# Threshold attention and a gated feed-forward: q and k loaded once and rearranged on the chip, in place of two shifted loads

## The chip, the cores and the metric

The kernel runs on one core of a Trainium2 chip. The metric is device microseconds (us) of one execution, start of the first instruction to end of the last. Before the change the median of three runs is 576.11 us (573.69 to 577.81). The profile shown is of one execution with a span of 573.6 us between its first and last instruction.

The engines are named as the profile names them: PE (TensorE matmul), PEld (its weight loads), DVE (VectorE), ACT (ScalarE), POOL (GpSimd) and SP (SyncE, which here only issues transfers). SPq and ACTq are their instruction queues as issuers of DMA.

## The reference

Eight batches, eight heads, 576 rows (tokens) of 64 numbers each. Attention keeps only the scores that lie within `tau` = 0.02 of the largest of their row; a feed-forward block follows.

```python
scores = q @ k.T / sqrt(64)                       # per batch and head, 576 x 576
thresh = max(scores, row) - tau
attn   = softmax(where(scores >= thresh, scores, -1e9))
x      = (attn @ v) -> [4608 tokens, 8 heads * 64]
xn     = x / sqrt(mean(x*x) + 1e-6) * rms_g
out    = (silu(xn @ w_gate) * (xn @ w_val)) @ w_out      # 512 -> 1536 -> 512
```

Inputs and output are float32.

## The kernel before

**Tiling.** Two heads form a pair (four pairs a batch). A chunk is 128 rows of q of one batch, four chunks a batch; the last 64 rows of two batches make one more chunk together. That is 36 chunks, and with four pairs each 144 steps. One step runs through these instructions:

- Scores: PE multiplies a chunk of q with all 576 k rows, each head on 64 of the 128 partitions of `qkt` (L687), into `s_ps`.
- DVE copies the scores, negated and scaled, to `ssb` (three buffers) and takes the row minimum, `mx` (L720).
- POOL adds tau: `nth` (L761), a tiny instruction.
- ACT pushes everything beyond the threshold far away (Prelu with a huge slope, L772, two a step) and takes the exponential, into `wsb` in float16 (L779, three buffers).
- The weights must be transposed for the next product. In the first 16 steps PE does it (L824); in the other 128 a transposing DMA does, from SP's queue (L839), into `wt` (five buffers).
- PE multiplies two steps' weights with v (L857 and L862); DVE divides by the row sums (L879, L881 or L886) into `xsb`.

After four pairs of a chunk, ACT squares (L903), POOL finds the root mean square and scales (L906, L908, L911: the norm chain), and SP issues a transposing DMA into `xnT` (L915). Four chunks (two at first) form a group for the feed-forward block: PE for gate (L974) and value (L979), ACT for tanh (L988), DVE for the products (L991, L996), PE for the output (L1045; L1020 in the last group), DVE or ACT for the copy out (L1058, L1060), and SP or ACT for the store (`store_blocks`, L948, for blocked batches). The feed-forward matmuls fill PE while the softmax chain runs.

**q and k.** For the scores they must lie with the 64 numbers of a head along partitions, so each has to be transposed. Batches 0 and 1 are transposed on PE (L338, L448). Batches 2 to 7 are "blocked": DVE's transpose turns each 32x32 block in place (block of partitions by 32 columns), and does not move blocks between groups of 32 partitions. A row of q has two halves of 32 numbers, so the second halves must already lie on another block of partitions than the first. The kernel before obtains that by loading every row twice: each block of 32 partitions holds 18 whole rows per partition (`RUN = 18`, 4608 bytes in one run), one copy (`e = 0`) stored 32 elements later than the other (`e = 1`). The reading view `kx`, `qx` takes 32 of each 64 columns at one place for all partitions, and so finds first halves on one block and second halves on the next:

```python
rows = slice(64 * h + 32 * e, 64 * h + 32 * e + 32)
at = WIDE * (1 - j) + 32 * (1 - e)
nc.sync.dma_start(out=qkx[rows, at:at + GROUP * RUN * D]..., in_=src[b, a0:a0 + GROUP]...)
```

A load covers two pairs of one side of the partitions; four loads (h, e) bring two pairs of k, four more those of q. There is one buffer for each of k and q, so the next two pairs' loads wait until the turns of the present two have read it (L373; turns at L387, L392 and L397, the last for q). Which rows sit where decides the row order of everything that follows, so v and the output are loaded and stored in the same order: v in four loads of 32 partitions a batch, the output in four stores of 32 rows a chunk.

**Order.** Every instruction is put in its engine's list by a planner that knows a cost for each (`COST`, `DMA_NS`), buffers, and a rank per kind of operation (`RANK`). The lists are fixed when the kernel is built, and each engine works strictly through its own. All loads and nearly all stores share SP's list with the transposing DMAs.

Of the kernel before, what the change touches and what calls it, by code (L numbers as in the profile page):

```python
# [9 lines left out]
FP16 = mybir.dt.float16  # L10
# [10 lines left out]
    sp=420.0, sp_v=600.0, sp_w=600.0, sp_tr=1300.0, sp_qk=680.0, sp_tl=630.0, sp_qb=600.0, turn=600.0, turn_t=210.0, turn_q=680.0,  # L21
)
DMA_NS = dict(qkb=750.0, qk=1250.0, tl=700.0, v=880.0, vt=350.0, wt=1700.0, xt=800.0, out=800.0, w=820.0, wo=2500.0)
# [3 lines left out]
    ACT={"emit_ffn/ev": 300, "emit_ffn/store": 50, "emit_ffn/tanh": -293, "emit_k_tail/ev": -150, "emit_q_tail/ev": -130, "emit_qk/ev": 320,  # L27
        "emit_softmax/ex2": -329.5, "emit_softmax/prelu": 80, "emit_x/sq": -310},
    DVE={"emit_av/half": -20, "emit_blocks/turn_k": 30, "emit_blocks/turn_kt": 30, "emit_blocks/turn_q": 68, "emit_burst/ttr": -40, "emit_ffn/ev":
        103, "emit_ffn/gate": -60, "emit_ffn/silu": -20, "emit_k_tail/ev": -120, "emit_qk/ev": -80, "emit_softmax/ev": 360},  # L30
    PE={"emit_av/fn": -270, "emit_burst/fn": -140, "emit_ffn/gmm": 19, "emit_ffn/omm": 21, "emit_ffn/vmm": -110, "emit_k_tail/tr": 240,
        "emit_q_tail/tr": -160, "emit_qk/tr": 90, "emit_softmax/tr": -120},
    POOL={"emit_softmax/nthr": -90, "emit_x/mean": -80, "emit_x/norm": -20, "round_/<lambda>": -30, "main/<lambda>": 690, "main/cast": -220},
# [115 lines left out]
def kernel(  # L149
# [12 lines left out]
    nc = tc.nc  # L162
# [16 lines left out]
    def ps(name, n):  # L179
# [10 lines left out]
    RUN = S // 32  # L190
    LEAD = TAIL // 32
    GROUP = 2
    WIDE = GROUP * RUN * D + 32
    qkx = sb("qkx", [128, 2 * WIDE])
    kx, qx = [qkx[:, WIDE * j + 32:WIDE * (j + 1)].rearrange("p (a r d) -> p a r d", a=GROUP, d=D)[:, :, :, 0:32] if 0 else
              bass.AP(tensor=qkx.tensor, offset=qkx.offset + WIDE * j + 32, ap=[list(qkx.ap[0]), [RUN * D, GROUP], [D, RUN], [1, 32]])
              for j in range(2)]
# [20 lines left out]
    esb = [sb(f"esb{i}", [128, S], FP16) for i in range(NES)]  # L218
# [139 lines left out]

    assert BLOCKED == 2 and WIDE < 1024 * NQK
    turned = []  # L360

    def emit_block_loads(b, g, prio):

        los = {}
        for j, src in ((1, k), (0, q)):
            before = turned[j] if turned else [x for t in tr_of for x in t[-NQK:]] + ([] if j else tail_load["use", 0])
            for h in range(2):
                for e in range(2):
                    def load(o, j=j, src=src, h=h, e=e):
                        rows = slice(64 * h + 32 * e, 64 * h + 32 * e + 32)  # L370
                        at = WIDE * (1 - j) + 32 * (1 - e)
                        a0 = NP * h + GROUP * g
                        nc.sync.dma_start(out=qkx[rows, at:at + GROUP * RUN * D].rearrange("s (a n) -> s a n", a=GROUP),  # L373
                                          in_=src[b, a0:a0 + GROUP].rearrange("a (s r) d -> s a (r d)", r=RUN))

                    pr = prio + BLOCK_STEP * len([x for y in los.values() for x in y])
                    los.setdefault(j, []).append(gated(add("SP", COST["sp_qb"], pr, before, load, dma=DMA_NS["qkb"], bulk=True), pr))
                    los[j][-1].lat = LAT_QB
        turned[:] = [[], []]
        return los  # L380

    def emit_blocks(b, p, prio, los):
        free = last_s.get(("k", b - 2, p), [])
        dst = qkt[b % 2][:, p]

        def turn_k(o):
            nc.vector.transpose(out=dst[:, TAIL:S].rearrange("p (c k d) -> p c k d", c=4, d=32),  # L387
                                in_=kx[:, p % GROUP, LEAD:RUN].rearrange("p (k c) d -> p c k d", c=4))

        def turn_kt(o):  # L390
            src = kx[:, p % GROUP, 0:LEAD]
            nc.vector.transpose(  # L392
                out=dst[:, 0:2 * S].rearrange("p (j n) -> p j n", j=2)[:, :, 0:TAIL].rearrange("p j (t d) -> p j t d", d=32),
                in_=bass.AP(tensor=src.tensor, offset=src.offset, ap=[list(src.ap[0]), [0, 2], list(src.ap[1]), list(src.ap[2])]))

        def turn_q(o):
            nc.vector.transpose(out=dst[:, S + TAIL:2 * S + TAIL].rearrange("p (r d) -> p r d", d=32), in_=qx[:, p % GROUP])  # L397

        tk = gated(add("DVE", COST["turn"], prio, los[1] + free, turn_k), prio)
        tt = gated(add("DVE", COST["turn_t"], prio, los[1] + free, turn_kt), prio)  # L400
        tq = gated(add("DVE", COST["turn_q"], prio, los[0] + free, turn_q), prio)
        turned[0].append(tq)
        turned[1] += [tk, tt]
        for c in range(4):
            qk_ready[b, p, c] = [tk, tt, tq]
        kt_ready[b, p] = []
# [155 lines left out]
    def emit_v(b, prio):  # L562
# [13 lines left out]
        for p in range(NP):  # L576
            pr = prio + 3 * p if b else (-25.0, -24.0, -21.0, -20.0)[p]
            n = len(v_cast)
            nat = vst[n % len(vst)]

            def load(o, p=p, nat=nat):
                nc.sync.dma_start(out=nat, in_=main[:, 2 * p:2 * p + 2])

            if b < BLOCKED:
                lo = [gated(add("SP", COST["sp_v"], pr, v_cast[n - len(vst):n - len(vst) + 1] if n >= len(vst) else [], load,
                                dma=DMA_NS['v'], bulk=True), pr)]
            else:
                nat = vst8.rearrange("q (h a) x -> q a h x", h=2)[:, p]
            if b >= BLOCKED and p == 0:
                lo = []  # L590
                for g in range(4):
                    def load_block(o, g=g):
                        at = LEAD + 4 * g
                        nc.sync.dma_start(out=vst8[32 * g:32 * g + 32].rearrange("s h (c d) -> s h c d", d=D),
                                          in_=v[b].rearrange("h (s r) d -> s h r d", r=RUN)[:, :, at:at + 4])

                    pl = pr + V_FROM + V_STEP * g
                    lo.append(gated(add("SP", COST["sp_v"], pl, v_cast[-NP:], load_block, dma=DMA_NS['v'], bulk=True), pl))
                    lo[-1].lat = LAT_V
            ca = add("POOL", COST["cast_v"], (pr + V_CAST if b >= BLOCKED else pr + 1 if b else p - 1.0), lo + free(p), round_(  # L600
                t[:, p, 0:8, 0:D].rearrange("q (c h) d -> q h c d", h=2),
                nat.rearrange("q h (c d) -> q h c d", d=D)))
            v_cast.append(ca)
            v_ready.setdefault((b, p), []).append(ca)
            if p == 0:
                def load_tail(o):
                    for e in range(2):
                        if b >= BLOCKED:
                            for t in range(LEAD):
                                at = 64 * e + 32 * t  # L610
                                nc.sync.dma_start(out=vtl[at:at + 32], in_=v[b, NP * e:NP * e + NP].rearrange(
                                    "a (s r) d -> r s a d", r=RUN)[t])
                            continue
                        nc.sync.dma_start(out=vtl[64 * e:64 * e + 64], in_=hv[e, MAIN:S])

                lt = gated(add("SP", (4 if b >= BLOCKED else 2) * COST["sp_tl"], pr + 0.3, vt_cast[-2:], load_tail, dma=DMA_NS['vt'], bulk=True), pr + 0.3)
# [228 lines left out]
    def emit_av(s):  # L845
# [31 lines left out]
        def half(_):  # L877
            o3 = ring[o.slot[0]][:, 0:4 * (D + 1)].rearrange("p (h d) -> p h d", d=D + 1)
            nc.vector.reciprocal(out=r, in_=o3[:, :, D])  # L879
            if bs[0] >= BLOCKED:  # L880
                nc.vector.tensor_tensor(  # L881
                    out=xsb[ci % 2].rearrange("p (h a d) -> p a h d", h=2, d=D)[:, 2 * hp:2 * hp + 2],
                    in0=o3[:, :, 0:D].rearrange("p (a h) d -> p a h d", h=2),
                    in1=r.rearrange("p (a h) -> p a h", h=2)[:, :, :, None].to_broadcast([128, 2, 2, D]), op=ALU.mult)
                return
# [59 lines left out]

    def store_blocks(b, oi, n, row, at, late):
        for i in range(n):
            (nc.scalar if late and i % 2 else nc.sync).dma_start(  # L948
                out=out[b * S:b * S + S].rearrange("(s r) d -> r s d", r=RUN)[row + i], in_=osb[oi][at + 32 * i:at + 32 * i + 32])

    def emit_ffn(slot, parts, ready_step, pace, streamed):
# [81 lines left out]
        for j, (ci, _) in enumerate(parts):  # L1033
# [28 lines left out]
            def store(o, oi=oi, kind=kind, b=b, c=c, late=late):  # L1062
                if kind == "m":
                    if b >= BLOCKED:
                        store_blocks(b, oi, 4, 4 * c, 0, late)
# [3 lines left out]
                else:  # L1069
                    for e in range(2):  # L1070
                        if 2 * b >= BLOCKED:
                            store_blocks(2 * b + e, oi, LEAD, MAIN // 32, 64 * e, False)
                            continue
                        r0 = (2 * b + e) * S
                        nc.sync.dma_start(out=out[r0 + MAIN:r0 + S], in_=osb[oi][64 * e:64 * e + 64])
# [5 lines left out]
            osb_use[oi] = add("ACT" if late else "SP", (2200.0 if b >= BLOCKED else COST["sp"]) if kind == "m" else 2100.0 if 2 * b >= BLOCKED else 1100.0, pr, [e], store,  # L1081
# [140 lines left out]
BLOCK_STEP = 0.6  # L1222
# [50 lines left out]
```

## Time and profile before

| what | value |
|---|---|
| median time | 576.11 us (573.69 to 577.81, three runs) |
| span of the profiled execution | 573.6 us, mean granted clock 0.988 |
| busy: PE / DVE / ACT / POOL | 529.8 (92%) / 468.0 (82%) / 445.2 (78%) / 129.5 us (23%) |
| DMA moved | 103.21 MB; SP's queue 100.18 MB, its packets 91.9% of 16 engines' span |
| q/k loads of blocked batches | 96 of 288 KB, median 5.3 (k) and 5.7 us (q) to landing |
| transposing DMAs | 128 for wt, median 4.6 us, and 36 for xnT, 4.2 us |
| turns (L387, L392, L397) | 24 of each at 698, 287 and 765 ns |

Shares of busy time are averages over stages that are limited by different things: until about 80 us the weights of the feed-forward block come in and are rounded, from 80 to 440 us the blocked batches' q and k come in, and after about 516 us only feed-forward work is left. So it is the stretches that have to be read, and in them the waits. DMA shares count the time that packets take, and packets overlap, so a share can exceed 1.

### The profile page before, as it was taken

What the parts mean: (1) busy time and instruction counts of PE and PEld (TensorE: products, weight loads), DVE (VectorE), ACT (ScalarE), POOL (GpSimd) and SP (SyncE); (2) the same over time, 40 slices, a digit from 0 to 9 for tenths busy, and PEclk for the clock granted to TensorE, in tenths of its full rate; (3) what the DMA queues carried; (4) which work ended last, traced back from release to release, by engine and by line L of the source; (5) the groups of instructions that cost most, each with busy time, mean ns of one, the idle gap of its engine ahead of it and who ended that gap; (6) DMA issues with size and microseconds to landing.
All of it is one profiled execution on the core that took longest, in us unless ns stands there. A gap on an engine that the chain in (4) does not pass through costs nothing.

```text
span 573.6 us, 14361 instructions
## 1 busy us (share of the span) xinstructions
PE 529.8 (92%) x5336; PEld 276.2 (48%) x5336; DVE 468.0 (82%) x1342; ACT 445.2 (78%) x648; POOL 129.5 (23%) x334
## 2 busy tenths in 40 slices
PE   8998999886999998989998989988989999999994
PEld 4666765443544444435453535443444454454441
DVE  4998988775999798989997989987789888866641
ACT  5998988678997998878986998886788999952210
POOL 2378402041221312113121311231120411111000
PEclk9999999988999999999999999998999999999998
DMA  8999999999799999999999999998999885761103
GB/s 195 242 262 277 202 158 211 196 223 218 154 214 200 204 202 171 205 219 215 192 217 213 183 206 178 226 197 182 195 199 224 149 131 111 128 113 44 31 19 93
DMA packets 222887, 103.21 MB, mean 180 GB/s; under 512 B 199264, under 2 KB 208992, under 8 KB 222816
## 3 DMA queue, kind: packets, MB, share of 16 engines
q1 hardware_dynamic: 219984, 100.18, 91.9%
q0 software_dynamic: 1600, 1.57, 1.9%
q8 instruction: 42, 0.69, 0.6%
q10 hardware_dynamic: 1232, 0.52, 0.4%
q14 instruction: 29, 0.24, 0.2%
HBM read 51.91 MB, written 9.44 MB: 107 GB/s over the span
## 4 chain that ended last, share of the span: by engine, by line
PE 41%; DMA 26%; ACT 17%; DVE 6%; issue 5%; POOL 3%; SPq 0%; ACTq 0%; DVEq 0%; POOLq 0%
DMA wt<-wsb 21%; PE s_ps L687 11%; ACT ssb L772 8%; PE ring L1045 8%; PE ring L974 7%; PE ring L979 6%; ACT wsb L779 6%; DVE ssb L720 4%; DMA xnT<-xn 2%; PE ring L862 2%; ACT th L988 2%; DMA stg<-in_moe_w_val_dram 2%; PE s_ps L1020 2%; PE ring L857 1%; PE s_ps L979 1%
## 5 line engine op out<-in xcount | busy, mean ns | idle before, releaser
L772 ACT ACTIVATE ssb<-ssb,nth 128x576 f32<-128x576 f32 x288 | 209.6, 765 | 23.4 <-POOL nth L761 22.9
L779 ACT ACTIVATE wsb<-ssb 128x1152 f16<-128x1152 f32 x144 | 166.8, 1159 | 30.6 <-DMA wt<-wsb 28.8
L720 DVE CUSTOM_DVE_ANT_0 ssb<-s_ps,zrow 128x576 f32<-128x576 f32 (+8 forms) x288 | 170.7, 635 | 9.3 <-PE s_ps L687 6.8
L687 PE MATMUL s_ps<-qkt 64*64 64x288 f32 (+9 forms) x2240 | 171.9, 415 | 5.0 <-DVE mxp L720 3.8
L974 PE MATMUL ring<-xnT,wg 128*128 128x512 f16 (+1 forms) x464 | 109.9, 360 | 5.5 <-DMA xnT<-xn 5.5
L687 PEld LDWEIGHTS s_ps<-qkt 64*64 64x64 f32 (+1 forms) x2240 | 80.9, 135 | 70.6 <-issue 27.6
L979 PE MATMUL ring<-xnT,wv 128*128 128x512 f16 (+1 forms) x456 | 107.9, 359 | 0.3 <-DVE hf L996 0.3
L988 ACT ACTIVATE th<-ring 128x512 f32<-128x512 f32 (+1 forms) x116 | 62.8, 542 | 44.2 <-PE ring L974 44.0
L991 DVE SCALAR_TENSOR_TENSOR sl<-th,ring 128x512 f32<-128x512 f32 (+1 forms) x116 | 71.9, 624 | 17.8 <-ACT th L988 17.7
L761 POOL TENSOR_SCALAR nth<-mx 128x2 f32<-128x2 f32 x144 | 31.0, 215 | 244.0 <-DVE mx L720 240.3
L720 DVE CUSTOM_DVE_ANT_0 ssb<-s_ps,zrow,mxp 128x128 f32<-128x128 f32 (+7 forms) x112 | 53.2, 510 | 21.2 <-PE s_ps L687 18.4
L974 PEld LDWEIGHTS <-wg 128*128 128x128 f16 x480 | 44.1, 98 | 54.6 <-issue 14.1
L979 PEld LDWEIGHTS <-wv 128*128 128x128 f16 x480 | 43.8, 98 | 55.0 <-issue 17.3
L862 PE MATMUL ring<-va,wt 128*128 128x65 f16 (+1 forms) x1280 | 53.5, 193 | 0.0
L857 PE MATMUL ring<-va,wt 128*128 128x130 f16 (+1 forms) x160 | 32.5, 227 | 20.5 <-DMA wt<-wsb 20.5
L862 PEld LDWEIGHTS <-wt 128*128 128x128 f16 (+1 forms) x1280 | 47.1, 100 | 4.3
L1045 PE MATMUL ring<-wo,hf 128*128 128x512 f16 x204 | 47.9, 379 | 0.0
L1045 PE MATMUL ring<-wo,stg 128*128 128x512 f16 x156 | 38.5, 392 | 0.0
L996 DVE TENSOR_TENSOR stg<-ring,sl 128x512 f16<-128x512 f32 (+1 forms) x57 | 35.5, 625 | 2.3
L996 DVE TENSOR_TENSOR hf<-ring,sl 128x512 f16<-128x512 f32 (+1 forms) x57 | 35.3, 623 | 2.1 <-PE ring L979 0.4
L857 PEld LDWEIGHTS <-wt 128*128 128x128 f16 (+1 forms) x160 | 14.2, 99 | 40.1 <-DMA wt<-wsb 23.7
L1045 PEld LDWEIGHTS <-hf 128*128 128x128 f16 x216 | 20.1, 98 | 24.6 <-issue 2.5
(69 smaller groups left out, 403.6 us busy)
## 6 DMA issues: line engine op xcount, KB each, us to landing
qkx<-in_k_dram SPq DMA_DIRECT2D x48, 288.0 KB, 5.3
qkx<-in_q_dram SPq DMA_DIRECT2D x48, 288.0 KB, 5.7
vst<-in_v_dram SPq DMA_DIRECT2D x32, 256.0 KB, 4.6
out_dram<-osb SPq DMA_DIRECT2D x98, 64.0 KB, 1.8
stg<-in_moe_w_gate_dram SPq DMA_DIRECT2D x6, 512.0 KB, 6.2
stg<-in_moe_w_val_dram SPq DMA_DIRECT2D x6, 512.0 KB, 6.3
wt<-wsb SPq DMA_TRANSPOSE x128, 4.6
out_dram<-osb SPq DMA_DIRECT2D x8, 256.0 KB, 3.6
```

Source lines behind the costliest of these rows:

```text
L687: nc.tensor.matmul(s_ps[h][rows, at:at + hi - lo], lhs(hs), k_of(bb, p, h)[hs, lo:hi], start=True, stop=True)
L720: nc.vector.tensor_tensor_reduce(out=ssb_of(s)[:, h, lo:hi], in0=s_ps[h][:, at:at + hi - lo], in1=zrow[:, lo:hi], scale=-1.0 / 8.0, scalar ...
L772: nc.scalar.activation(out=sb_[:, h], in_=sb_[:, h], func=PRELU, scale=-1.0, bias=nth[m][:, h:h + 1], **PRELU_KW)
L779: nc.scalar.activation(out=wsb[s % NW], in_=sb_, func=AF.Exp)
L857: nc.tensor.matmul(ring[o.slot[0]][rs, at:at + 2 * (D + 1)], w[:, 4, rs], va[vi][:, p, 8:10].rearrange("p e d -> p (e d)"), start=True, st ...
L862: nc.tensor.matmul(ring[o.slot[0]][rs, at:at + D + 1], w[:, 5 * h + j, rs], va[vi][:, p, 2 * j + h], start=False, stop=(h == 1 and j == 3))
L974: nc.tensor.matmul(ring[o.slot[0]][:, 0:n], wg[d][:, fs], xnT[slot][:, d, 0:n], start=(d == 0), stop=(d == 3))
L979: nc.tensor.matmul(ring[o.slot[0]][:, 0:n], wv[d][:, fs], xnT[slot][:, d, 0:n], start=(d == 0), stop=(d == 3))
L988: nc.scalar.activation(out=th[i][:, 0:n], in_=ring[g.slot[0]][:, 0:n], func=AF.Tanh, scale=0.5)
L991: nc.vector.scalar_tensor_tensor(out=sl[i][:, 0:n], in0=th[i][:, 0:n], scalar=1.0, in1=ring[g.slot[0]][:, 0:n], op0=ALU.add, op1=ALU.mult)
L996: nc.vector.tensor_tensor(out=hf[hi][:, 0:n], in0=ring[vv.slot[0]][:, 0:n], in1=sl[i][:, 0:n], op=ALU.mult)
L1045: nc.tensor.matmul(ring[(first or o).slot[0]], hf[hs[fc][0]][:, 128 * j:128 * (j + 1)], wo[:, fc], start=(fc == 0), stop=(fc == NFC - 1))
```

## The change

Every row of q and k is now loaded once, nine whole rows on each of 128 partitions (`RUN = 9`, 2304 bytes in one run): 64 partitions hold one head, the other 64 the other head of the pair. A load covers two pairs, and there are two buffers (`g`), so that all four pairs of a batch have a place. Both halves of a row now lie on the same partition. To put the halves on the blocks of partitions where the turn needs them, POOL swaps the second halves of one block of 32 partitions with the first halves of the next, by way of a `spare` tile: three copies for each half of a load. The turns by DVE stay, with other shapes.

The row order changes with it (64 x 9 in place of 32 x 18), so v comes in two loads of 64 partitions a batch, its last rows in two loads and not four, and the output in two stores of 64 rows a chunk. Heads of a pair are now neighbours, so the output product needs no form of its own for blocked batches. An unused buffer (`esb`) makes room for `spare`. The planner's costs and ranks are set anew, which changes the order of the lists of all engines.

```diff
-    RUN = S // 32
+    RUN = S // 64
...
-    qkx = sb("qkx", [128, 2 * WIDE])
+    qkx = sb("qkx", [128, 2 * 2 * GROUP * RUN * D])
+    nat = qkx.rearrange("p (g j a r d) -> p g j a r d", g=2, j=2, a=GROUP, d=D)
+    spare = sb("spare", [128, GROUP * RUN * 32]).rearrange("p (a r d) -> p a r d", a=GROUP, d=32)
...
     def emit_block_loads(b, g, prio):
...
+                nc.sync.dma_start(out=own.rearrange("p a r d -> p a (r d)"),
+                                  in_=src[b, a0:a0 + 2 * GROUP].rearrange("(a h) (m r) d -> h m a (r d)", h=2, r=RUN))
...
             for h in range(2):
-                for e in range(2):
...
+                lower, upper = slice(64 * h, 64 * h + 32), slice(64 * h + 32, 64 * h + 64)
+                moves = [(spare[upper], own[lower, :, :, 32:64]), (own[lower, :, :, 32:64], own[upper, :, :, 0:32]),
+                         (own[upper, :, :, 0:32], spare[upper])]
+                last = [lo] + spare_use[-1:]
+                for dst, at in moves:
+                    def swap(o, dst=dst, at=at):
+                        nc.gpsimd.tensor_copy(out=dst, in_=at)
+
+                    last = [add("POOL", COST["swap"], prio + SWAP_AT, last, swap)]
...
         def turn_q(o):
-            nc.vector.transpose(out=dst[:, S + TAIL:2 * S + TAIL].rearrange("p (r d) -> p r d", d=32), in_=qx[:, p % GROUP])
+            nc.vector.transpose(out=dst[:, S + TAIL:2 * S + TAIL], in_=nat[:, g, 1, a].rearrange("p r n -> p (r n)"))
...
-    def store_blocks(b, oi, n, row, at, late):
-        for i in range(n):
...
                     if b >= BLOCKED:
-                        store_blocks(b, oi, 4, 4 * c, 0, late)
+                        rows = out[b * S:b * S + S].rearrange("(m r) d -> r m d", r=RUN)
+                        for i in range(2):
+                            (nc.scalar if late and i else nc.sync).dma_start(out=rows[2 * c + i], in_=osb[oi][64 * i:64 * i + 64])
```

More of the change, by code (lines that the diff above doesn't have):

```diff
@@ L20 @@
     pool_tiny=302.0, pool_mean=944.0, pool_dma=880.0, cast_v=620.0, cast_vt=475.0, cast_w=665.0,
-    sp=420.0, sp_v=600.0, sp_w=600.0, sp_tr=1300.0, sp_qk=680.0, sp_tl=630.0, sp_qb=600.0, turn=600.0, turn_t=210.0, turn_q=680.0,
+    sp=420.0, sp_v=600.0, sp_w=600.0, sp_tr=1300.0, sp_qk=680.0, sp_tl=630.0, sp_qb=600.0, swap=790.0, turn=600.0, turn_t=210.0, turn_q=680.0,
 )
-DMA_NS = dict(qkb=750.0, qk=1250.0, tl=700.0, v=880.0, vt=350.0, wt=1700.0, xt=800.0, out=800.0, w=820.0, wo=2500.0)
+DMA_NS = dict(qkb=1600.0, qk=1250.0, tl=700.0, v=880.0, vt=350.0, wt=1700.0, xt=800.0, out=800.0, w=820.0, wo=2500.0)
 SWITCH = 125.0
 RANK = dict(
[L27 to L33, printed above, removed]
+    ACT={"emit_ffn/ev": 400, "emit_ffn/store": 40, "emit_ffn/tanh": -350, "emit_k_tail/ev": -230, "emit_q_tail/ev": -70, "emit_qk/ev": 390,
+        "emit_softmax/prelu": 170, "emit_x/sq": -320},
+    DVE={"emit_av/half": -39, "emit_blocks/turn_k": 90, "emit_blocks/turn_kt": 140, "emit_blocks/turn_q": 280, "emit_burst/ttr": -50, "emit_ffn/ev":
+        185, "emit_ffn/gate": -20, "emit_ffn/silu": -44, "emit_k_tail/ev": -110, "emit_qk/ev": -120, "emit_softmax/ev": 250},
+    PE={"emit_av/fn": -340, "emit_burst/fn": -110, "emit_ffn/gmm": 21, "emit_ffn/omm": 22, "emit_ffn/vmm": -20, "emit_k_tail/tr": 220,
+        "emit_q_tail/tr": -70, "emit_softmax/tr": -110},
+    POOL={"emit_block_loads/swap": 60, "emit_softmax/nthr": -240, "emit_x/mean": -110, "emit_x/norm": -50, "round_/<lambda>": 60, "main/<lambda>":
+        760, "main/cast": -300},
 )
@@ L189 @@
     wo = sb("wo", [128, NFC, DM], FP16)
-    RUN = S // 32
-    LEAD = TAIL // 32
+    RUN = S // 64
     GROUP = 2
-    WIDE = GROUP * RUN * D + 32
-    qkx = sb("qkx", [128, 2 * WIDE])
-    kx, qx = [qkx[:, WIDE * j + 32:WIDE * (j + 1)].rearrange("p (a r d) -> p a r d", a=GROUP, d=D)[:, :, :, 0:32] if 0 else
-              bass.AP(tensor=qkx.tensor, offset=qkx.offset + WIDE * j + 32, ap=[list(qkx.ap[0]), [RUN * D, GROUP], [D, RUN], [1, 32]])
-              for j in range(2)]
+    qkx = sb("qkx", [128, 2 * 2 * GROUP * RUN * D])
+    nat = qkx.rearrange("p (g j a r d) -> p g j a r d", g=2, j=2, a=GROUP, d=D)
+    spare = sb("spare", [128, GROUP * RUN * 32]).rearrange("p (a r d) -> p a r d", a=GROUP, d=32)
     qkn = [qkx[:, 1024 * i:1024 * (i + 1)].rearrange("p (j c h d) -> p j c h d", j=2, c=4, d=D) for i in range(NQK)]
@@ L217 @@
     nth = [sb(f"nth{i}", [128, 2]) for i in range(6)]
-    esb = [sb(f"esb{i}", [128, S], FP16) for i in range(NES)]
+    esb = [sb(f"esb{i}", [128, S], FP16) for i in range(NES if set(WAYS) != {"pp"} else 0)]
     NW = 3
@@ L357, in emit_qk @@
             qk_ready[b, p, c] = done
-    assert BLOCKED == 2 and WIDE < 1024 * NQK
-    turned = []
+    assert BLOCKED == 2
+    turned, spare_use = {}, []
     def emit_block_loads(b, g, prio):
-        los = {}
+        done = {}
         for j, src in ((1, k), (0, q)):
-            before = turned[j] if turned else [x for t in tr_of for x in t[-NQK:]] + ([] if j else tail_load["use", 0])
-            for h in range(2):
-                for e in range(2):
[L369 to L380, printed above, removed]
@@ new lines, in emit_block_loads, with load @@
+            before = turned[g, j] if (g, j) in turned else [x for t in tr_of for x in t[-NQK:]] + (tail_load["use", 0] if g else [])
+            own = nat[:, g, 1 - j]
+            def load(o, src=src, own=own):
+                a0 = 2 * GROUP * g
+                nc.sync.dma_start(out=own.rearrange("p a r d -> p a (r d)"),
+                                  in_=src[b, a0:a0 + 2 * GROUP].rearrange("(a h) (m r) d -> h m a (r d)", h=2, r=RUN))
+            pr = prio + BLOCK_STEP * (1 - j)
+            lo = gated(add("SP", COST["sp_qb"], pr, before, load, dma=DMA_NS["qkb"], bulk=True), pr)
@@ new lines, in emit_block_loads @@
+            lo.lat = LAT_QB
+            done[j] = []
+            for h in range(2):
+                lower, upper = slice(64 * h, 64 * h + 32), slice(64 * h + 32, 64 * h + 64)
[6 more added lines that the diff above has]
+                    last = [add("POOL", COST["swap"], prio + SWAP_AT, last, swap)]
+                spare_use.append(last[0])
+                done[j] += last
@@ L382, in emit_blocks @@
+            turned[g, j] = []
+        return done
     def emit_blocks(b, p, prio, los):
@@ L384, in emit_blocks @@
         dst = qkt[b % 2][:, p]
+        g, a = divmod(p, GROUP)
         def turn_k(o):
-            nc.vector.transpose(out=dst[:, TAIL:S].rearrange("p (c k d) -> p c k d", c=4, d=32),
-                                in_=kx[:, p % GROUP, LEAD:RUN].rearrange("p (k c) d -> p c k d", c=4))
+            nc.vector.transpose(out=dst[:, TAIL:S].rearrange("p (c k n) -> p c k n", c=4, n=64),
+                                in_=nat[:, g, 0, a, 0:RUN - 1].rearrange("p (k c) n -> p c k n", c=4))
         def turn_kt(o):
[L391 to L394, printed above, removed]
+            src = nat[:, g, 0, a, RUN - 1]
+            nc.vector.transpose(out=dst[:, 0:2 * S].rearrange("p (j n) -> p j n", j=2)[:, :, 0:TAIL],
+                                in_=bass.AP(tensor=src.tensor, offset=src.offset, ap=[list(src.ap[0]), [0, 2], [1, TAIL]]))
         def turn_q(o):
-            nc.vector.transpose(out=dst[:, S + TAIL:2 * S + TAIL].rearrange("p (r d) -> p r d", d=32), in_=qx[:, p % GROUP])
+            nc.vector.transpose(out=dst[:, S + TAIL:2 * S + TAIL], in_=nat[:, g, 1, a].rearrange("p r n -> p (r n)"))
         tk = gated(add("DVE", COST["turn"], prio, los[1] + free, turn_k), prio)
@@ L401, in emit_blocks @@
         tq = gated(add("DVE", COST["turn_q"], prio, los[0] + free, turn_q), prio)
-        turned[0].append(tq)
-        turned[1] += [tk, tt]
+        turned[g, 0].append(tq)
+        turned[g, 1] += [tk, tt]
         for c in range(4):
@@ L578, in emit_v, with load @@
             n = len(v_cast)
-            nat = vst[n % len(vst)]
-            def load(o, p=p, nat=nat):
-                nc.sync.dma_start(out=nat, in_=main[:, 2 * p:2 * p + 2])
+            nat_v = vst[n % len(vst)]
+            def load(o, p=p, nat_v=nat_v):
+                nc.sync.dma_start(out=nat_v, in_=main[:, 2 * p:2 * p + 2])
             if b < BLOCKED:
@@ L587, in emit_v @@
             else:
-                nat = vst8.rearrange("q (h a) x -> q a h x", h=2)[:, p]
+                nat_v = vst8[:, 2 * p:2 * p + 2]
             if b >= BLOCKED and p == 0:
                 lo = []
-                for g in range(4):
+                for g in range(2):
                     def load_block(o, g=g):
-                        at = LEAD + 4 * g
-                        nc.sync.dma_start(out=vst8[32 * g:32 * g + 32].rearrange("s h (c d) -> s h c d", d=D),
-                                          in_=v[b].rearrange("h (s r) d -> s h r d", r=RUN)[:, :, at:at + 4])
+                        nc.sync.dma_start(out=vst8[64 * g:64 * g + 64].rearrange("m h (c d) -> m h c d", d=D),
+                                          in_=v[b].rearrange("h (m r) d -> m h r d", r=RUN)[:, :, 4 * g:4 * g + 4])
                     pl = pr + V_FROM + V_STEP * g
-                    lo.append(gated(add("SP", COST["sp_v"], pl, v_cast[-NP:], load_block, dma=DMA_NS['v'], bulk=True), pl))
+                    lo.append(gated(add("SP", COST["sp_v"], pl, v_cast[-NP:], load_block, dma=2 * DMA_NS['v'], bulk=True), pl))
                     lo[-1].lat = LAT_V
@@ L601, in emit_v @@
                 t[:, p, 0:8, 0:D].rearrange("q (c h) d -> q h c d", h=2),
-                nat.rearrange("q h (c d) -> q h c d", d=D)))
+                nat_v.rearrange("q h (c d) -> q h c d", d=D)))
             v_cast.append(ca)
@@ L607, in load_tail @@
                     for e in range(2):
[L608 to L616, printed above, removed]
+                        nc.sync.dma_start(out=vtl[64 * e:64 * e + 64], in_=hv[e, MAIN:S] if b < BLOCKED else v[b].rearrange(
+                            "(a e) (m r) d -> e r m a d", e=2, r=RUN)[e, RUN - 1])
+                lt = gated(add("SP", 2 * COST["sp_tl"], pr + 0.3, vt_cast[-2:], load_tail, dma=DMA_NS['vt'], bulk=True), pr + 0.3)
                 for e in range(2):
@@ L879, in half @@
             nc.vector.reciprocal(out=r, in_=o3[:, :, D])
[L880 to L885, printed above, removed]
             nc.vector.tensor_tensor(
@@ L944 @@
     clock = [0.0]
-    def store_blocks(b, oi, n, row, at, late):
-        for i in range(n):
-            (nc.scalar if late and i % 2 else nc.sync).dma_start(
-                out=out[b * S:b * S + S].rearrange("(s r) d -> r s d", r=RUN)[row + i], in_=osb[oi][at + 32 * i:at + 32 * i + 32])
     def emit_ffn(slot, parts, ready_step, pace, streamed):
@@ L1070, in store @@
                     for e in range(2):
-                        if 2 * b >= BLOCKED:
-                            store_blocks(2 * b + e, oi, LEAD, MAIN // 32, 64 * e, False)
-                            continue
                         r0 = (2 * b + e) * S
-                        nc.sync.dma_start(out=out[r0 + MAIN:r0 + S], in_=osb[oi][64 * e:64 * e + 64])
+                        dst = out[r0 + MAIN:r0 + S] if 2 * b < BLOCKED else out[r0:r0 + S].rearrange("(m r) d -> r m d", r=RUN)[RUN - 1]
+                        nc.sync.dma_start(out=dst, in_=osb[oi][64 * e:64 * e + 64])
             e = add("DVE" if on_dve else "ACT", 600.0 if on_dve else 476.0, pr - PUSH[0],
@@ L1080, in emit_ffn @@
             late = late and kind == "m"
-            osb_use[oi] = add("ACT" if late else "SP", (2200.0 if b >= BLOCKED else COST["sp"]) if kind == "m" else 2100.0 if 2 * b >= BLOCKED else 1100.0, pr, [e], store,
+            osb_use[oi] = add("ACT" if late else "SP", (1100.0 if b >= BLOCKED else COST["sp"]) if kind == "m" else 1100.0, pr, [e], store,
                               dma=DMA_NS['out'])
@@ L1221 @@
 BLOCKED = 2
-BLOCK_STEP = 0.6
+BLOCK_STEP = 3.0
+SWAP_AT = 4.0
 V_STEP = 1.0
```

## The prediction

> **What bounds the kernel now.** I read the engine shares first, then stretches of the span, then the waits of the middle stretch, then the DMA answers for that stretch and for a quiet one. All "before" figures are from a profiled execution with a span of 573.6 us.
>
> Busy time by stretch (columns: stretch, its length, busy us of PE, PEld, DVE, ACT, POOL with instruction counts, granted clock, DMA share, GB/s):
>
> ```profile
> core 0: us, PE busy (x) PEld busy (x) DVE busy (x) ACT busy (x) POOL busy (x), PEclk, DMA share, GB/s
> 0.00:80.00 80.00, 73.35 (x858) 49.42 (x862) 64.31 (x185) 67.34 (x108) 37.78 (x81) 1.00 1.04 225
> 80.00:440.00 360.00, 331.47 (x3473) 166.97 (x3465) 312.22 (x930) 299.83 (x428) 74.73 (x207) 0.99 1.09 201
> 440.00:574.00 134.00, 124.99 (x1013) 59.80 (x1013) 91.45 (x229) 78.02 (x115) 17.04 (x46) 0.99 0.51 96
> ```
>
> PE is nearest to its limit. Of its 43.8 us of idle time 28.5 (360 - 331.47) lie in 80-440, the stretch in which blocked q and k are loaded and turned; 6.7 are the start and 8.6 the end. In 80-440 the packets in flight fill more than the 16 DMA engines' time (share 1.09, packets overlapping); after 440, with no more q/k loads, the share halves and PE has no gap worth naming until 565.6. The waits of 80-440 (us in total, times, longest):
>
> ```profile
> POOL nth L761 <- DVE mx L720: 178.7, 78, 6.6
> ACT wsb L779 <- DMA wt<-wsb: 27.0, 20, 3.3
> PE ring L857 <- DMA wt<-wsb: 19.8, 20, 2.7
> ACT ssb L772 <- POOL nth L761: 16.8, 21, 2.5
> ACT th L988 <- PE ring L974: 14.6, 12, 2.3
> ```
>
> So 19.8 of PE's 28.5 us end with a transposed weight block (wt) landing, and ACT loses 27.0 to the same transfers, because a wsb buffer is free only once it has been transposed. Now the DMA queue in 80-440 and in the quiet stretch 460-500 (packets, MB, share; issues and median us to landing):
>
> ```profile
> q1 hardware_dynamic: 152167, 71.80, 108.2%
> qkx<-in_q_dram SPq DMA_DIRECT2D x47, 288.0 KB, 5.8
> qkx<-in_k_dram SPq DMA_DIRECT2D x44, 288.0 KB, 5.2
> wt<-wsb SPq DMA_TRANSPOSE x101, 4.9
> xnT<-xn SPq DMA_TRANSPOSE x25, 4.5
> ```
>
> ```profile
> q1 hardware_dynamic: 16925, 4.84, 74.1%
> wt<-wsb SPq DMA_TRANSPOSE x12, 3.4
> ```
>
> The same transpose lands in 3.4 us when no loads run beside it and in 4.9 when they do. That 1.5 us is what the change can get at.
>
> [...] 128x512 casts take 628 ns and 64x256 casts 406, so 0.87 ns [...] an element and 184 ns fixed. [...]
>
> **The change, part by part.**
>
> *q/k loads.* 96 loads of 288 KB (every byte twice) become 24 of 576 KB: 28.3 MB become 14.2. Packet time in 80-440 is 1.082 x 360 = 390 us. In 460-500 it is 0.741 x 40 = 29.6 us for 4.84 MB, nearly all transposes: 6.1 us per MB. The 101 wt and 25 xnT transposes of 80-440 are 33.1 MB, so 202 us; the other 38.7 MB take 188, 4.8 per MB. The 91 q/k loads there (26.8 MB) take 129. Halved at the same price, 65 are saved[...]. The share falls from 1.08 to 0.83-0.90. On a line through (0.74, 3.4 us) and (1.08, 4.9), 0.865 gives 3.95: a wt lands about 0.95 us sooner. PE's 20 waits average 1.0 us, so most shrink to little; since the order on each engine is fixed and ACT (83% busy) and DVE (87%) must now deliver sooner, I take 12 of 19.8. PE's xnT waits there (4.7 in all, L974) give 2 more. Ends: 5 and 22.
>
> *Swaps.* 48 halves of loads times three copies = 144 GpSimd copies of 32x576. From the casts' line: 184 + 576 x 0.87 = 685 ns, plus about 0.09 us from one dependent POOL instruction to the next (norm chain at 189 us): 0.77 us, 111 in all[...]. POOL goes from 75 to about 186 of 360 us: not full. But it is in order, and a swap waits for its load and for the swap before it. Queued behind are nth (L761, for which ACT's prelu waits) and the norm chain (for which the xnT transpose waits). By the built order 101 nth lie between first and last swap; 48 have no swap between them and the nth before, 20 have four to six. Steps come every 3.6 us, and five swaps last 3.9. I put 1.5 us of lateness on those 20 and 0.4 on the other 33: 43 us. Three ssb buffers take up part of it, and PE has feed-forward matmuls meanwhile; I take a third for ACT (14) and a third of that for the end: +5. Ends: 0 and +29.
>
> *Turns.* Same three per pair, same element counts: nothing. They now follow six swaps (4.6 us) per load, hidden while the second group buffer lets loads start earlier; before, a late q load at 400 us stood on the chain.
>
> *Queue.* SP's list falls from 475 to 327 instructions; 72 q/k issues at about 0.48 us and some 76 of v and stores at about 0.42 free about 65 us. SP mostly waits for ACT (98.0 us for L772 alone), so this only makes transposes leave sooner; counted within the 12. At the end it counts by itself: the last matmul ends at 565.6, SP issues six 32-row stores from 566.24 to 569.95 and the last two from 570.05 to 570.89. Half as many: three in 1.9 us and one in 0.4, ending at about 568.5. -2 (1 to 3).
>
> *The rest.* The two output multiplies (L881, L886) both take 425 ns: nothing. esb is not used. PE's rows barely change (7186 to 7194), but with other priorities 264 instead of 228 matmuls stand after the last weight-value product. At about 0.216 us that is 7.8 us of work moved behind 516 us; it is free if the softmax part really ends earlier, and lost if not.
>
> Sum: -12 - 2 + 5 - 2 = -11; 576.1 - 11 = **565**.
>
> **Rivals.** (A) The sum, 565. (B) PE fills nearly all: 80-440 keeps 8 of its 28.5 us of gaps and POOL costs nothing: 576.1 - 20 - 2 = 554. For it: after 440 PE ran without gaps. Against: ACT and DVE are at 83% and 87% there. (C) GpSimd becomes the gate: [...] with -12 - 2 - 2 the time is 589. For it: ACT already waits 16.8 us for nth with POOL at 21%, and a late load now holds nth up too. Against: POOL keeps half its time free. (D) The wait changes its name: 12 saved at wt, 12 lost at nth: 576.1 - 2 = 574, or with the 7.8 us of moved matmuls uncovered 582.
>
> **How the numbers follow.** A 0.48, B 0.22, C 0.18, D 0.12. The time is A's, 565. The range, 549 to 586, takes in most of B, all of D, the near part of C, and A with either end of its DMA term. Faster by over 1% (under 570.3): nearly all of A and all of B, 0.68. Within 1%: most of D and a little of A, 0.13. Slower: C and the rest of D, 0.19.
>
> **What would show it.** Right: in the middle stretch the DMA share is 0.83-0.95, wt lands in about 4 us, PE <- wt is under 9 us, swaps run at 0.7-0.85 us, ACT <- nth is 25-35. Wrong: a DMA share still above 1.0 (the bytes were cheap), PE <- wt unchanged (transposes leave late, not land late), ACT <- nth above 50 (C), or mean L720 or turn times up [...].

## The result, and the profile after

The changed kernel takes 538.85 us (median of four runs, 537.68 to 540.73), beside 576.25 for the kernel before on the same chip: a ratio of 0.936, 95% interval 0.931 to 0.941. The forecast, 565 with a range down to 549, had the direction and missed the size by a factor of more than three (37 us, not 11). The profiled execution spans 539.0 us where it spanned 573.6. Each run further down has its ratio to the kernel before on its own chip, where that kernel took 573.2 to 575.7 us, so small differences between medians of different runs have to be read with the intervals of the ratios. Ratios leave out slow executions, which only run 8 had (six of twenty; its median of 572.8 us is 571.5 without them).

Busy time of the changed kernel by stretch, with the columns as before (stretch, length, busy us of PE, PEld, DVE, ACT, POOL, granted clock, DMA share, GB/s):

```profile
0.00:80.00 80.00, 73.76 (x858) 49.54 (x859) 64.28 (x185) 68.32 (x108) 43.66 (x90) 1.00 1.06 229
80.00:440.00 360.00, 354.55 (x3891) 181.05 (x3889) 339.31 (x1028) 333.43 (x476) 173.47 (x368) 1.00 0.94 176
440.00:539.00 99.00, 93.49 (x607) 43.85 (x605) 61.73 (x131) 42.54 (x66) 7.71 (x21) 0.99 0.38 74
```

In the middle stretch PE's idle time fell from 28.5 to 5.5 us. VectorE and ACT, which were busy for 87% and 83% of it, are now busy for 94% and 93%: they had been waiting too. POOL more than doubled, to 48%, and the DMA share is below 1. The waits of this stretch, changed kernel:

```profile
ACT ssb L775 <- POOL nth L764: 12.6, 20, 2.4
...
ACT th L980 <- PE ring L966: 8.3, 11, 1.9
...
PE ring L860 <- DMA wt<-wsb: 2.3, 4, 1.0
ACT wsb L782 <- DMA wt<-wsb: 2.1, 2, 1.2
PE ring L966 <- DMA xnT<-xn: 2.1, 2, 1.1
```

PE's waits for transposed weights went from 19.8 us to 2.3 and ACT's from 27.0 to 2.1. ACT's wait for nth, which the swaps were to lengthen, went down from 16.8 to 12.6. The chain of work that ended last, in the same stretch, begins with these shares, the kernel before first:

```profile
by line: DMA wt<-wsb 33.7%; PE s_ps L687 9.9%; ACT ssb L772 9.0%; ACT wsb L779 7.2%; issue 6.2%; PE ring L1045 5.6%; DVE ssb L720 4.6%; PE ring L974 4.1%; DMA xnT<-xn 3.5%; ACT th L988 3.2%; PE ring L979 2.7%; PE ring L862 1.6%; DMA qkx<-in
by line: PE s_ps L690 17.4%; DMA wt<-wsb 12.8%; DVE ssb L723 10.7%; PE ring L966 9.6%; PE ring L971 8.6%; PE ring L1037 8.0%; ACT ssb L775 4.6%; ACT wsb L782 3.8%; issue 3.5%; PE ring L865 3.4%; DVE sl L983 3.4%; DMA xnT<-xn 3.1%; DVE stg L
```

Weight transposes held a third of it and now hold an eighth. Some that stood on it before took 8.4 to 9.0 us to land (issued at 99, 172, 245 and 384 us), far more than the median of 4.9 from which the prediction worked. The DMA queue of the same stretch:

```profile
q1 hardware_dynamic: 167501, 62.74, 93.4%
qkx<-in_q_dram SPq DMA_DIRECT2D x11, 576.0 KB, 4.8
...
qkx<-in_k_dram SPq DMA_DIRECT2D x10, 576.0 KB, 4.9
wt<-wsb SPq DMA_TRANSPOSE x113, 3.9
```

Twice as many bytes in a load land no later than before (4.8 and 4.9 us; before, 288 KB took 5.8 for q and 5.2 for k), and a weight transpose lands in 3.9 us (before 4.9; the prediction said 3.95). 113 of them fit into the 360 us that held 101. So one step takes 360/113 = 3.19 us in place of 3.56.

**A way to read this that the prediction did not use:** divide the stretch's packet time by its steps and set it beside PE's busy time for a step. Before: 1.082 x 360 / 101 = 3.86 us of DMA a step, against 331.47/101 = 3.28 of PE. After: 0.934 x 360 / 113 = 2.98 against 354.55/113 = 3.14. Packets overlap, so these are not times on a path. They also seem to grow with crowding: run 1 below leaves out 0.13 MB a step, which at the prediction's 4.8 us per MB is 0.64 us, and the figure fell by 0.79 (to 3.06). But their order changed: before, the transfers' figure was above PE's; after, PE's is the longer one. That the stretch before ran at the pace of the transfers is a guess from this, which runs 1, 8 and 9 test.

**Half-clock stretches.** The page's clock row rounds this away, so here is the kernel before in pieces of 4 us around two of its gaps (piece, length, PE busy, granted clock, DMA share, GB/s):

```profile
112.00:116.00 4.00, 2.07 (x46) 1.00 1.20 207
116.00:120.00 4.00, 4.00 (x28) 0.57 1.11 225
...
128.00:132.00 4.00, 1.27 (x15) 1.00 1.11 183
132.00:136.00 4.00, 2.14 (x49) 1.00 1.16 177
136.00:140.00 4.00, 3.19 (x12) 0.61 1.24 276
```

After these pieces, which PE left about half idle or more, the clock is at half (0.50 in each microsecond from 117 to 119 and from 137 to 140) for some 3.4 us ((1 - 0.57) x 4 / 0.5). The kernel before has three such stretches between 80 and 440 us, the third after a gap that begins at 385 us; the changed kernel has none there. Each costs 1.7 us of PE's work: 5.1 us, on top of the gaps themselves. A half-idle piece does not always bring one. Here are two that did not, each with the piece after it, first from the kernel before and then from run 1 (where the gap is a single one of 2.73 us):

```profile
252.00:256.00 4.00, 2.03 (x19) 1.00 1.24 202
256.00:260.00 4.00, 4.00 (x48) 1.00 1.12 246
...
120.00:124.00 4.00, 1.79 (x26) 1.00 1.07 199
124.00:128.00 4.00, 2.88 (x42) 1.00 1.22 202
```

The single gaps before the three stretches were short: 1.93 us before the first, 2.73 us at most.

### The profile page after: what moved, and what is told of

The parts are those of the page before. It is cut to its first block, busy times and chain, and to the rows that moved or that the text cites. A ratio compares the mean times of both kernels' runs of the same rounds, so it can differ in the third digit from the quotient of the medians.

```text
span 539.0 us, 14315 instructions
## 1 busy us (share of the span) xinstructions
PE 521.8 (97%) x5352; PEld 274.4 (51%) x5352; DVE 465.3 (86%) x1342; ACT 444.3 (82%) x648; POOL 224.8 (42%) x478
## 4 chain that ended last, share of the span: by engine, by line
PE 58%; DVE 16%; DMA 13%; ACT 9%; issue 3%; POOL 0%; DVEq 0%; SPq 0%; ACTq 0%; POOLq 0%
PE s_ps L690 17%; PE ring L966 11%; PE ring L971 10%; PE ring L1037 9%; DMA wt<-wsb 9%; DVE ssb L723 8%; ACT ssb L775 4%; PE ring L865 3%; ACT wsb L782 3%; DVE sl L983 3%; DMA qkx<-in_q_dram 2%; DMA xnT<-xn 2%; PE s_ps L1012 2%; DVE stg L988 2%; PE ring L860 1%
## 5 line engine op out<-in xcount | busy, mean ns | idle before, releaser
L723 DVE CUSTOM_DVE_ANT_0 ssb<-s_ps,zrow 128x576 f32<-128x576 f32 (+8 forms) x288 | 169.2, 635 | 8.4 <-PE s_ps L690 7.1
L966 PE MATMUL ring<-xnT,wg 128*128 128x512 f16 (+1 forms) x456 | 107.1, 357 | 2.5 <-DMA xnT<-xn 2.1
L980 ACT ACTIVATE th<-ring 128x512 f32<-128x512 f32 (+1 forms) x114 | 61.6, 541 | 40.6 <-PE ring L966 40.0
L723 DVE CUSTOM_DVE_ANT_0 ssb<-s_ps,zrow,mxp 128x128 f32<-128x128 f32 (+7 forms) x112 | 52.9, 509 | 15.9 <-PE s_ps L690 13.4
L865 PE MATMUL ring<-va,wt 128*128 128x65 f16 (+1 forms) x1280 | 51.8, 193 | 0.0
L865 PEld LDWEIGHTS <-wt 128*128 128x128 f16 (+1 forms) x1280 | 46.4, 100 | 4.3
L988 DVE TENSOR_TENSOR stg<-ring,sl 128x512 f16<-128x512 f32 (+1 forms) x59 | 36.7, 627 | 2.2
L1037 PE MATMUL ring<-wo,stg 128*128 128x512 f16 x156 | 36.8, 379 | 0.0
L988 DVE TENSOR_TENSOR hf<-ring,sl 128x512 f16<-128x512 f32 (+1 forms) x55 | 33.9, 623 | 1.6
L383 POOL COPY spare<-qkx 32x576 f32<-32x576 f32 x48 | 31.7, 660 | 8.1 <-DMA qkx<-in_k_dram 3.0
L903 POOL TENSOR_SCALAR irm<-ssq 128x1 f32<-128x1 f32 x36 | 6.9, 192 | 66.4 <-ACT xn L900 65.7
```

Of the source, the lines that this page charges most:

```text
L723: nc.vector.tensor_tensor_reduce(out=ssb_of(s)[:, h, lo:hi], in0=s_ps[h][:, at:at + hi - lo], in1=zrow[:, lo:hi], scale=-1.0 / 8.0, scalar ...
L865: nc.tensor.matmul(ring[o.slot[0]][rs, at:at + D + 1], w[:, 5 * h + j, rs], va[vi][:, p, 2 * j + h], start=False, stop=(h == 1 and j == 3))
L966: nc.tensor.matmul(ring[o.slot[0]][:, 0:n], wg[d][:, fs], xnT[slot][:, d, 0:n], start=(d == 0), stop=(d == 3))
L980: nc.scalar.activation(out=th[i][:, 0:n], in_=ring[g.slot[0]][:, 0:n], func=AF.Tanh, scale=0.5)
L988: nc.vector.tensor_tensor(out=hf[hi][:, 0:n], in0=ring[vv.slot[0]][:, 0:n], in1=sl[i][:, 0:n], op=ALU.mult)
L1037: nc.tensor.matmul(ring[(first or o).slot[0]], hf[hs[fc][0]][:, 128 * j:128 * (j + 1)], wo[:, fc], start=(fc == 0), stop=(fc == NFC - 1))
```

## The experiments

Three theories stood against each other. BYTES: the second copy of q and k kept the DMA engines so full that the transposing DMAs landed late and set the pace. ORDER: the new ranks made a better order. QUEUE: fewer instructions on SP's list let transposes leave sooner. Then what the swaps cost, what the second buffer does, and whether wide loads are cheaper.

**1. The kernel before without the second copy.** Nothing else changes; the order stays, there are no swaps. In this run and the next the scores of the blocked batches use stale numbers where the second copy is missing, and the columns of `qkx` from 4096 on are cleared once at the start.

```diff
                     def load(o, j=j, src=src, h=h, e=e):
...
+                        if e:
+                            return
```

> The kernel before, with the second copy of q and k (e = 1) not loaded at all; everything else, order included, as before (the scores of blocked batches then use stale numbers). Loads fall from 96 to 48 issues and from 28.3 to 14.2 MB; there are no swaps. Theory BYTES (loads crowd the transposing DMAs, PE's waits for wt and the clock dips behind them follow): 576 falls to 550-560, DMA share in 80-440 near 0.9, PE waits for wt under 8 us. Theory ORDER (the gain comes from the new ranks): 570-577. Theory QUEUE (the number of issues on SP's list): as BYTES here, but not in the next run.

Measured: 540.98 us, ratio 0.942 (0.935 to 0.948). The middle stretch and its queue:

```profile
80.00:440.00 360.00, 355.64 (x3847) 183.65 (x3843) 338.25 (x1024) 331.20 (x473) 83.67 (x232) 1.00 0.96 176
```

```profile
q1 hardware_dynamic: 165290, 62.84, 95.3%
...
wt<-wsb SPq DMA_TRANSPOSE x112, 3.9
```

PE 355.64, 112 transposes at 3.9 us: the changed kernel's stretch, with the old order and half of POOL's work. VectorE and ACT are busy for 94% and 92% here too. PE has no wait for wt left, and no transfer is among the pieces of the stretch's chain that were listed. BYTES had expected 550-560 and was itself too careful. Whether stale numbers change PE's pace was not tried by itself; runs 8 and 9 vary the bytes with the right numbers.

**2. The same number of issues, half the bytes.** The second copy shrinks to 256 bytes for each partition.

```diff
+                        if e:
+                            nc.sync.dma_start(out=qkx[rows, at:at + D],
+                                              in_=src[b, a0].rearrange("(s r) d -> s (r d)", r=RUN)[:, 0:D])
+                            return
```

> As the run above, but the second copy is cut to 256 bytes for each partition and not left out: still 96 issues on SP's list, bytes almost halved (14.4 MB). BYTES: within 3 us of the run above. QUEUE: back near 576. ORDER: 570-577 in both.

Measured: 543.85 us, ratio 0.947 (0.941 to 0.952). 48 more issues bring 2.9 us by the medians, and the intervals of the two runs overlap; QUEUE falls as the main cause.

**3. and 4. The ranks exchanged.** The changed kernel with the old ranks, and the kernel before with the new ones.

```diff
-RANK = dict(... as in the kernel itself ...)
+RANK = dict(... as in the other kernel ...)
```

> The changed kernel with the ranks of the kernel before (the swap's own rank kept), so the planner makes another order. BYTES: 539-548, most of the gain stays. ORDER: 560 or more, most of the gain goes.

> The kernel before with the ranks of the changed kernel. BYTES: 570-582, no gain. ORDER: below 560.

Measured: 552.42 us (ratio 0.961, 0.955 to 0.968) and 575.95 (1.001, 0.998 to 1.004). The new ranks alone do nothing for the old transfers. With the new loads and the swaps they are worth 13.6 us, more than BYTES allowed. Three half-clock stretches between 120 and 360 us make 5.1 of these (mean clock of the execution 0.988, changed kernel 0.998); the changed kernel has none there. It is not that the order counts as soon as transfers stop setting the pace: run 1 has the old order and takes 541. The new ranks suit the new loads and swaps; run 1 with the new ranks was not tried.

**5. The changed kernel without the swap copies.**

```diff
-                        nc.gpsimd.tensor_copy(out=dst, in_=at)
+                        pass
```

> The changed kernel without the 144 copies on GpSimd (the turns then read halves in the wrong places); order and loads as in the changed kernel. Theory FREE (the swaps hide beside other work): 536-540, within 2 us of 538.9. Theory GATE (they delay nth and cost what the prediction charged, 5 us, or more): 534 or less.

Measured: 539.85 us, ratio 0.936 (0.931 to 0.941), the changed kernel's own. FREE holds: 144 copies of 0.66 us, 95 us of POOL's time, cost nothing that can be measured in this order.

**6. The swap copies made twice.**

```diff
                         nc.gpsimd.tensor_copy(out=dst, in_=at)
+                        nc.gpsimd.tensor_copy(out=dst, in_=at)
```

> The changed kernel with every swap copy made twice: 288 copies of 0.66 us, the turns read the same. Theory SLACK (GpSimd has room): 539-544. Theory EDGE (the swaps just fit, since they take 173 of 360 us with the rest in the middle stretch): 550 or more, with ACT's wait for nth doubled.

Measured: 599.96 us, ratio 1.047 (1.044 to 1.050): 61 us slower than the changed kernel, for another 94 us of copies. Its middle stretch and its longest wait there:

```profile
80.00:440.00 360.00, 321.07 (x3304) 166.71 (x3306) 293.64 (x880) 282.80 (x403) 239.98 (x454) 0.97 0.79 153
```

```profile
ACT ssb L776 <- POOL nth L765: 65.4, 38, 5.8
```

EDGE holds. POOL is busy for 67%, the DMA engines are less full than in any other run here, and ACT waits five times as long for nth. The copies (L383 and L384) hold 36.5% of the chain in this stretch (12.1 + 11.9 + 6.3 + 6.2), and the clock falls to 0.97. This is the prediction's rival C, with twice the copies: the swaps are free as they stand, and as many again are not. Where between the two the edge lies was not tried. POOL became the gate here at an average of two thirds.

**7. One group buffer in place of two.**

```diff
-            own = nat[:, g, 1 - j]
+            own = nat[:, 0, 1 - j]
...
-        turned[g, 0].append(tq)
+        turned[0, 0].append(tq)
```

> The changed kernel with one group buffer for q and k in place of two: the next two pairs' loads wait for the present two pairs' turns, as they did before the change. The planner knows, so the order shifts a little. Theory BUFFER (the second group hides the load and the swaps): 545 or more. Theory BYTES (only traffic matters): 537-543.

Measured: 546.17 us, ratio 0.949 (0.943 to 0.955), so about 7 us above the changed kernel. ACT's wait for nth doubles, to 25.1 us; that the swaps, coming later, hold nth up is a likely reading and was not traced. BUFFER holds for the kernel with swaps; run 1, with one buffer and no swaps, takes 541.

**8. and 9. Bytes put back, over 128 partitions.** With one group buffer the other half of `qkx` is free, and loads can go there a second time: all of them, or those of k alone.

```diff
+                extra[0] += 1
+                nc.sync.dma_start(out=nat[:, 1, extra[0] % 2].rearrange("p a r d -> p a (r d)"),
+                                  in_=src[b, a0:a0 + 2 * GROUP].rearrange("(a h) (m r) d -> h m a (r d)", h=2, r=RUN))
```

> The run with one group buffer, and every q/k load of the blocked batches issued a second time into the half that is then free: 28.3 MB again, in 48 loads over 128 partitions. BYTES with equal prices: back to 565-578. BYTES with wide loads cheaper[...]: 548-560. If bytes are not the cause: as the run with one buffer.

> The run with one group buffer, with k alone loaded twice: 21.2 MB of q/k traffic, half way between 14.2 (546.2 us) and 28.3 (572.8 us). Theory LINE (each byte costs alike): 557-562. Theory KNEE (bytes are free until the DMA share of 80-440 nears 1, then gaps and half-clock stretches come): 546-552.

Measured: all twice, 572.76 us, ratio 0.992 (0.989 to 0.995); k twice, 552.39, ratio 0.965 (0.962 to 0.967). Run 8 lies where wide and narrow loads cost alike (565-578) and not where wide ones are cheaper (548-560). Against one copy (0.949) the first 7.1 MB add 1.6% and the next 7.1 MB 2.8%. That bends as KNEE has it, less sharply than either expectation: a bit above KNEE's range, below LINE's. With all loads twice:

```profile
80.00:440.00 360.00, 333.26 (x3479) 168.68 (x3478) 311.11 (x929) 298.38 (x426) 172.34 (x355) 0.97 1.01 204
```

PE's middle stretch is that of the kernel before (331.47), with half the issues and with wide loads; the mean clock there is down to 0.97. Weight transposes hold 24.2% of its chain. Packet time for a step, worked out as above, orders the runs that differ in bytes: 2.98 us (changed kernel 538.9, one buffer 546.2), 3.06 (half the bytes, 541.0), 3.23 (k twice, 552.4), 3.59 (all twice, 572.8), 3.86 (before, 576.3). It says nothing of runs held up by something else: with the swaps made twice it is 2.93, at 600 us.

**10. Loads cut into four of 32 partitions.**

```diff
+                for i in range(4):
+                    h, m0 = divmod(i, 2)
+                    nc.sync.dma_start(out=own[32 * i:32 * i + 32]..., in_=src[b, ...]...[h, 32 * m0:32 * m0 + 32])
```

> The changed kernel with each 576 KB load cut into four of 32 partitions (144 KB each): same bytes, 96 issues again. Theory WIDTH [...]: DMA share in 80-440 up from 0.93 to about 1.0 and 541-550. Otherwise 538-541.

Measured: 544.00 us, ratio 0.943 (0.938 to 0.948). WIDTH stands for narrow loads that cost more for each byte. The time is in its range but not for its reason: the DMA share of the stretch is 92.7%, no higher than with wide loads (93.4%). So loads of 32 partitions did not cost more a byte here. The four loads are issued one after another and reach all 128 partitions between them, as in the kernel before; a narrow load on its own was not tried. By the ratios the intervals overlap with the changed kernel's, and where the 5 us come from, issues or the two half-clock stretches of this run (at 24 and 287 us; mean clock 0.993), is not settled.

**11. The old ranks, and no swap copies.**

> The changed kernel with the old ranks and without the swap copies (the turns then read halves in the wrong places). The old ranks gave 552.4 with swaps, and ACT waited 32.1 us for nth there. Theory PLACE (the new ranks are worth 13 us because they put the swaps where they do not hold up nth): 538-544. Theory PLAN (the new ranks suit the rest better too): 548-553.

Measured: 548.14 us, ratio 0.956 (0.955 to 0.958). PLAN rather than PLACE: of the 13.6 us that separate the ranks, 4.3 at most by the medians lie in where the swaps stand (552.4 against 548.1; the intervals overlap, so even these are not shown) and the rest elsewhere. Why this kernel, with the old ranks and no swaps, is still slower than run 1 (541.0) was not traced.

**12. Stores of 32 rows again.** Runs 11 and 12 are the edits of run 3 with run 5, and `range(4)` in place of `range(2)` in the store.

> The changed kernel with each main store of the blocked batches cut into four of 32 rows, as before the change: some 50 more issues on SP's list. Theory TAIL (the issues at the very end count, 2 us): 540-542. Theory NONE: 538-540. Theory QUEUE (issues count throughout): 545 or more.

Measured: 541.21 us, ratio 0.945 (0.942 to 0.948), 2.4 us above the changed kernel by medians and 5 by ratios. After 440 us PE is idle for 6.7 us (99.2 - 92.46) against 5.5: 1.2 us of the cost is at the end, behind the last matmul. TAIL has the size by the medians; the rest of the cost has no place yet.

## Why the prediction was wrong

Its sum, term by term, beside what the two profiles show (spans 573.6 and 539.0, so -34.6 in all):

| term | predicted | measured | from |
|---|---|---|---|
| PE waits for wt, 80-440 | -12 | -17.5 | 19.8 to 2.3 |
| PE waits for xnT, 80-440 | -2 | -2.6 | 4.7 to 2.1 |
| other PE gaps, 80-440 | 0 | -3.0 | rest of 28.5 to 5.5 |
| swaps | +5 | 0 | run 5 |
| end | -2 | -3.1 | idle after 440: 8.6 to 5.5 |
| PE's own busy time | not in the sum | -8.0 | 529.8 to 521.8 |
| start | 0 | -0.4 | 6.6 to 6.2 |

- *The bytes* were the right cause: fewer of them (62.74 MB on SP's queue in 80-440, before 71.80), and transposes land sooner (3.9 us, before 4.9). The packet share was forecast at 0.83-0.90 for the old pace and came out at 0.934, with 12% more steps in the stretch. The landing of 3.95 us (3.9) is in part luck: the prediction's line from share to landing gives 4.3 us at 0.934.
- *The step that failed* is the one after it, and it comes to 5.5 us of the 23.6 that lie between -11 and -34.6: "since the order on each engine is fixed and ACT (83% busy) and DVE (87%) must now deliver sooner, I take 12 of 19.8". It read those shares as limits. They were low because both engines lost time to the same transfers: they rose to 93% and 94%, and to 92% and 94% in run 1, where nothing but the second copy is gone. Runs 1, 8 and 9 show that the transfers set the pace of the stretch, so nearly all its gaps could go, not a part of one group of waits. The other gaps, put at nothing, are 3.0 us more of the same mistake.
- *Left out,* and the largest single term: PE's busy time was held fixed, and fell by 8.0 us; 5.1 of these are the three half-clock stretches that followed gaps, the rest is not traced.
- *Mis-sized:* the swaps, +5 where run 5 finds nothing. A copy takes 0.66 us, near the 0.685 forecast from GpSimd's casts (L570 of the kernel before, 628 and 406 ns), but the forecast lateness did not reach ACT: its wait for nth was to be 25-35 us and is 12.6 (13.2 without the swaps). Run 6 shows that the danger was real at twice the copies. The +29 behind rival C's 589 was the author's estimate of what dearer copies would cost; no copy of the changed kernel took over 0.67 us.
- *The price of width:* that wide loads cost less for each byte, which gave the lower end of the forecast share (0.83), was the author's estimate and was not shown: run 10 moves the same bytes in narrow loads at about the same DMA share (92.7%, wide 93.4%), run 1 reaches the same landing with them (3.9 us), and run 8's wide loads cost what equal prices give (572.8 us, in 565-578).
- *The end*, -2, was of the right size: the time behind the last matmul fell from 8.0 to 5.5 us, and run 12 puts 1.2 of these 2.5 down to the number of stores. The table's -3.1 takes in the other idle time after 440 us.
- *Rivals:* B (554, chance 0.22) had the gaps nearly right and lacked the clock; C came true only with twice the copies; D did not, since both waits fell. The 36 matmuls moved behind the last weight-value product were covered, since the softmax part did end earlier: its last product starts at 476.2 us in place of 516.1, and PE has no listed wait after 440 us.

## What to carry to other kernels

This is one kernel, so these are things to try first. Where a DMA share is at or above 1 over a long stretch, sum the packet time of one step and compare it with the busiest engine's time for one step. If it is larger, as here, the busy shares of the other engines may be no limits and the listed waits may share one cause; a run that leaves bytes out tells. A PE gap of 1.9 to 2.7 us was followed by a half-clock stretch of 3.4 us three times here and not always, so a change that removes gaps may gain more than the gaps (5.1 us more here). An engine that is half idle (POOL, busy for 48% of the stretch) took 95 us of copies for nothing here and had no room for as much again (600 us): a doubled copy of the suspected cost shows whether there is slack.

## What was not expected of the hardware

- Half-clock stretches of 3.4 us followed pieces in which PE was about half idle, with no single gap over 2.73 us (kernel before, 112 and 128 us). Other such pieces had none after them, one with a gap of 2.73 us (run 1, 120 us). That gaps bring them on rests on their coming together here, and was not tried by itself; what decides is open.
- GpSimd's plain copy of 32x576 float32 from one block of 32 partitions to the next took 0.66 us, whether it moved rows with a step (660 and 661 ns) or from the packed spare tile (663).
- VectorE's turns and minima did not slow beside more than twice the GpSimd work in the middle stretch (173.47 us, before 74.73): L723 means 751 ns for 576 elements (752 before), the q turns 756 (765).
